# Decay attention and two feed-forward products on one core: order of scalings, weight loads, reads of h, and who stores

## The chip, the core and the metric

The kernel runs on one core of a Trainium2 chip. The core has a matrix engine (TensorE; PE in the profile, PEld for its weight loads), three engines for elementwise work (VectorE, DVE; ScalarE, ACT; GpSimd, POOL) and SyncE (SP), which here only issues DMAs. Each engine works through its own instructions in order and waits at semaphores for the others; DMAs run beside them. The metric is the time of one execution on the device in microseconds, given as the median of several runs.

## The reference

Inputs are float64 arrays in memory for the weights that are unpacked below; the result is float32.

```python
scores = q @ k.T / sqrt(64)                      # 4 x 8 heads, 576 positions, 64 wide
cum    = cumsum(log(clip(f, 1e-4, 1)))
scores = where(causal, -1e9, scores + cum[:, None] - cum[None, :])
attn   = softmax(scores)                         # + 1e-9 under the division
x      = (attn @ v), heads side by side          # 2304 tokens x 512
h      = x @ w_in                                # 512 -> 2048
g      = h * tanh(softplus(h))                   # Mish
y      = g @ w_out                               # 2048 -> 512
out    = max(y @ w1, y @ w2, y @ w3) @ w_out2    # 512 -> 768 -> 512
```

## The kernel before, in words

Products are made in three matmuls of rounded halves (`mm3`: high x high, high x low, low x high), so each operand is first split into a high half (a rounding copy) and a low half (a subtraction), by `split`. Weights lie in memory as 64-bit numbers; `load_f32` brings both 32-bit words of each and puts a float32 together with four DVE steps (lines 156, 159, 162, 166; for w_in a fifth step, line 153, runs on ACT). The raw words have two buffers (`wr`).

Attention goes through 16 pairs of heads (4 batches x 4 pairs), each in two units (`g` 0: the first 256 query rows, `g` 1: the other 320). `load` issues the DMAs of one pair: q, k, v and the cumulated decay, which is spread over the partitions (`cb`), and masks copies of it with three selects on POOL. `prep` splits and transposes q and k. `scores` makes the scores of a unit's tiles (4, or 5 with the last 64 rows of both heads as one tile `P_None`), subtracts decay and finds the minimum on DVE, takes exponentials and sums on ACT; when all tiles are done, two small DVE steps make the reciprocals of the sums and POOL scales the tiles. `av`, one unit later, transposes P (`pp`), splits it (`TA`, `TB`), multiplies by v and stores the result to `x_d` in blocks of 256 tokens.

The first product, `h_steps`, is woven into it: as soon as a block of x is complete, `load_x` reads and splits it, and for each of 8 slices of w_in (`fp`) 24 matmuls make a tile of h, which ACT or DVE in turn copies (`he`, three buffers) and SP stores to `h_d`. Slices of w_in come from `load_w_in`, two groups a slice. When attention is over, 24 of the 72 tiles of h are still to be made, and `load_w_out` unpacks w_out beside them.

The second product goes over 5 blocks of h (four of 512 tokens, one of 256) and, in each, over 16 parts of 128 rows: `load_g` reads a part, applies Mish on ACT, copies the high half on ACT and subtracts on DVE; four buffers each for `g`, `gh`, `gl`. After the last part ACT and DVE copy the four tiles of y (`ze`) and SP stores them to `z_d`. The weights of the third stage (`load_w2`) are unpacked beside it. The third stage then takes the rest of the time.

Order: the program is laid out once, when it is built. A planner goes through the traced instructions by priority (the place in which they were traced; `tc.high_priority(n)` puts them n places forward) and by its own estimate of when inputs and buffers are there, and so fixes the order of each engine and of each DMA queue. Attention is traced with 3000 places (`AHEAD`) of priority. On the chip an instruction whose input is late holds up whatever stands behind it on its engine.

Of the kernel before, what the change touches and what calls it, by code (L numbers as in the profile page):

```python
# [9 lines left out]
F32 = mybir.dt.float32  # L10
# [57 lines left out]
def tile_decay_attention__mish_ff__max3_ff(  # L68
# [74 lines left out]

    def load_f32(pool, srcs, bufs=None, abs_eng="dve", raw="wr"):
# [4 lines left out]
        for i, src in enumerate(srcs):  # L149
            nc.sync.dma_start(r[:, i].rearrange("p n w -> p (n w)"), src.bitcast(I32))  # L150
# [118 lines left out]
    def load(b, hp):  # L269
# [14 lines left out]
        for n, src, dst in ((2, 0, 5), (1, 3, 2), (1, 4, 4)):  # L284
            nc.gpsimd.affine_select(
                out=c2[:, :, dst:dst + n, :], in_=c2[:, :, src:src + n, :], pattern=[[0, 2], [0, n], [-1, 128]],
                compare_op=ALU.is_ge, fill=-1e30, base=0, channel_multiplier=1,
            )
# [4 lines left out]
        nc.gpsimd.tensor_tensor(out=c4[:, 512:S], in0=c4[:, 512:S], in1=mask4, op=ALU.add)  # L293
# [16 lines left out]
    def prep(J):  # L310
# [35 lines left out]
        split_raw(J["vs"], raw[2], "act")  # L346
        J.update(q=(qh, ql), q4=last, k=kk)
# [13 lines left out]
    def scores(J, g):  # L361
# [11 lines left out]
        made = []  # L373
        for ci, (h, qt) in enumerate(tiles):
# [12 lines left out]
            for pi, (c0, w) in enumerate([(0, wd)] if qt < 4 else [(0, 288), (288, 288)]):  # L387
# [6 lines left out]
                    scale=-scale, scalar=(3e38 if pi == 0 else mn[:, ci:ci + 1]),  # L394
                    op0=ALU.add, op1=ALU.min, accum_out=mn[:, ci + pi:ci + pi + 1],
                )
            cl = ci + (qt == 4)
            nc.scalar.activation(  # L398
                Pt, Pt, AF.Exp, scale=-1.0, bias=mn[:, cl:cl + 1], accum_out=sm[:, ci:ci + 1],
            )  # L400
        nt = len(tiles)
        nc.vector.tensor_scalar(rr[:, :nt], sm[:, :nt], 1e-9, None, op0=ALU.add)
        nc.vector.reciprocal(rr[:, :nt], rr[:, :nt])  # L403
        for ci, Pt in enumerate(made):
            nc.gpsimd.tensor_scalar(Pt, Pt, rr[:, ci:ci + 1], 1.0, op0=ALU.mult, op1=ALU.mult)  # L405
        return P

    def av(J, g, P):
# [86 lines left out]
    def h_steps():  # L495
# [9 lines left out]
        for n, (i, fp) in enumerate(order):  # L505
# [48 lines left out]
    at.close()  # L554

# [51 lines left out]
    def load_g(ib, fp, a):  # L607
        n = blocks1[ib][1]
        g = gp_.tile([128, n], F32, name="g", tag="g")
        nc.sync.dma_start(g, h_d[ib][fp][:, a, :])  # L610
        nc.scalar.activation(g, g, AF.Mish)  # L611
        gh = gp_.tile([128, n], F32R, name="gh", tag="gh")
        gl = gp_.tile([128, n], F32R, name="gl", tag="gl")
        split(gh, gl, g, "act", "dve")
        return gh, gl

    wgen3 = load_w2()
    todo = [(ib, fp, a) for ib in range(len(blocks1)) for fp in range(NFP) for a in range(2)]
    ahead = [load_g(*todo[0]), load_g(*todo[1])]
    for step, (ib, fp, a) in enumerate(todo):  # L620
# [3 lines left out]
        g = ahead.pop(0)  # L624
        if step + 2 < len(todo):
            ahead.append(load_g(*todo[step + 2]))
        final = fp == NFP - 1 and a == 1
# [97 lines left out]
```

## Time and profile before

| | us |
|---|---|
| median of 3 runs | 1039.22 (1038.8 to 1040.48) |
| the profiled execution | 1036.78 |
| its span, first to last instruction | 1034.9 |
| TensorE busy / weight loads | 957.5 / 844.8 |
| VectorE busy | 509.5 |
| ScalarE busy | 425.6 |
| GpSimd busy | 379.9 |

The profile gives for each engine when it was busy and, for idle time before an instruction, what ended it (the releaser). Matmuls overlap, so a busy TensorE is not one at its peak. The granted clock of TensorE is a share of 2.4 GHz; it has two levels, 1.0 and 0.5. The rows below are from this execution; L123 is a line of the kernel.

### The profile page before, as it was taken

The numbers are of one execution on the slowest core, as the hardware profiler recorded it, in microseconds if no ns is written. First come the engines' busy times: TensorE is split into PE (matmuls) and PEld (weight loads), VectorE is DVE, ScalarE is ACT, GpSimd is POOL, SyncE is SP. The second block draws the span as 40 slices with busy tenths as digits, with TensorE's granted clock in tenths as the row PEclk, the third lists the DMA queues.
The fourth block names the chain that finished last, engine by engine and source line by source line (L and its number), as shares of the span: only waits on it lengthen the run. The fifth ranks groups of instructions, "written<-read, shape, count | busy, mean of one in ns | idle before, by whom it ended". The sixth has DMA issues, their size and how long they took to land.

```text
span 1034.9 us, 15873 instructions
## 1 busy us (share of the span) xinstructions
PE 957.5 (93%) x5756; PEld 844.8 (82%) x5756; DVE 509.5 (49%) x1103; ACT 425.6 (41%) x936; POOL 379.9 (37%) x437
## 2 busy tenths in 40 slices
PE   4777789989998999899699989998999999999998
PEld 4655679989997999799688768778988888888886
DVE  4798885554555555599855776652211111111110
ACT  5777666565656566441133444434211211211111
POOL 6676784445445542365432423320111001011010
PEclk8888889999998999999899999998999999999999
DMA  6644544345344431485545555643300100200101
GB/s 158 175 145 143 174 155 129 120 131 150 119 129 120 139 107 63 146 285 168 175 141 195 180 185 163 203 134 102 103 21 1 61 21 1 82 1 1 41 0 41
DMA packets 106445, 119.15 MB, mean 115 GB/s; under 512 B 33984, under 2 KB 79552, under 8 KB 106368
## 3 DMA queue, kind: packets, MB, share of 16 engines
q1 hardware_dynamic: 106368, 118.15, 37.0%
q8 instruction: 45, 0.74, 0.3%
q14 instruction: 32, 0.26, 0.1%
HBM read 85.01 MB, written 33.10 MB: 114 GB/s over the span
## 4 chain that ended last, share of the span: by engine, by line
PE 54%; DMA 18%; DVE 17%; issue 4%; ACT 3%; POOL 3%; SPq 2%; DVEq 0%; POOLq 0%; ACTq 0%
PE g L179 7%; PE g L178 7%; PE g L177 7%; DMA wr<-in_moe_w_dram 5%; PE h L177 4%; PE h L178 4%; PE h L179 4%; DMA wr<-in_moe_w_out_dram 4%; DVE wt L162 3%; PE av L437 3%; PE pp L424 3%; PE sc L357 3%; DMA cb<-cum_d 3%; PE o L177 2%; PE o L179 2%
## 5 line engine op out<-in xcount | busy, mean ns | idle before, releaser
L177 PE MATMUL h<-xh,wi 128*128 128x256 f32 x576 | 168.5, 294 | 13.0 <-ACT he L527 7.9
L178 PE MATMUL h<-xl,wi 128*128 128x256 f32 x576 | 167.4, 291 | 1.9 <-POOL xl L142 1.9
L179 PE MATMUL h<-xh,wi 128*128 128x256 f32 x576 | 166.9, 290 | 0.0
L142 POOL TENSOR_TENSOR hl<-mx,hh 128x512 fp32r<-128x512 f32 x27 | 36.5, 1352 | 279.1 <-ACT hh L136 279.1
L177 PE MATMUL g<-yh,wm 128*128 128x512 f32 (+1 forms) x360 | 134.3, 373 | 0.0
L179 PE MATMUL g<-yh,wm 128*128 128x512 f32 (+1 forms) x360 | 134.3, 373 | 0.0
L178 PE MATMUL g<-yl,wm 128*128 128x512 f32 (+1 forms) x360 | 134.3, 373 | 0.0
L177 PE MATMUL y<-gh,wo 128*128 128x512 f32 (+1 forms) x320 | 118.6, 375 | 6.9 <-ACT gh L136 5.0
L177 PEld LDWEIGHTS h<-xh,wi 128*128 128x128 f32 x576 | 112.1, 195 | 15.2 <-ACT he L527 8.8
L178 PE MATMUL y<-gl,wo 128*128 128x512 f32 (+1 forms) x320 | 119.0, 373 | 2.9 <-DVE gl L142 2.8
L179 PE MATMUL y<-gh,wo 128*128 128x512 f32 (+1 forms) x320 | 118.2, 371 | 0.0
L178 PEld LDWEIGHTS h<-xl,wi 128*128 128x128 f32 x576 | 112.5, 195 | 3.2 <-POOL xl L142 2.1
L179 PEld LDWEIGHTS h<-xh,wi 128*128 128x128 f32 x576 | 112.2, 195 | 0.4
L611 ACT ACTIVATE g<-g 128x512 f32<-128x512 f32 (+1 forms) x80 | 46.8, 588 | 123.9 <-DMA g<-h_d 117.4
L681 DVE TENSOR_TENSOR mx<-g,mx 128x512 f32<-128x512 f32 x27 | 18.7, 692 | 156.3 <-PE g L179 156.3
L424 PE MATMUL pp<-ident,P 128*128 128x128 f32 x320 | 69.9, 314 | 21.9 <-POOL P L405 19.8
L398 ACT ACTIVATE P<-P,mn 128x128 f32<-128x128 f32 (+3 forms) x128 | 71.2, 557 | 39.2 <-DVE mn L392 38.5
L178 PEld LDWEIGHTS g<-yl,wm 128*128 128x128 f32 x360 | 67.9, 189 | 13.3
L179 PEld LDWEIGHTS g<-yh,wm 128*128 128x128 f32 x360 | 67.9, 189 | 13.2
L177 PEld LDWEIGHTS g<-yh,wm 128*128 128x128 f32 x360 | 67.9, 189 | 13.1
L405 POOL TENSOR_SCALAR P<-P,rr 128x128 f32<-128x128 f32 (+3 forms) x128 | 68.0, 550 | 25.7 <-DVE rr L403 12.5
L177 PEld LDWEIGHTS y<-gh,wo 128*128 128x128 f32 x320 | 61.3, 192 | 18.4 <-ACT gh L136 6.4
(101 smaller groups left out, 1982.9 us busy)
## 6 DMA issues: line engine op xcount, KB each, us to landing
h_d<-he SPq DMA_DIRECT2D x72, 256.0 KB, 3.5
g<-h_d SPq DMA_DIRECT2D x64, 256.0 KB, 3.2
wr<-in_moe_w_out_dram SPq DMA_DIRECT2D x22, 512.0 KB, 4.0
wr<-in_moe_w_dram SPq DMA_DIRECT2D x24, 384.0 KB, 3.2
cb<-cum_d SPq DMA_DIRECT2D x64, 128.0 KB, 3.2
wr<-in_moe_w_in_dram SPq DMA_DIRECT2D x32, 256.0 KB, 3.5
cb<-cum_d SPq DMA_DIRECT2D x32, 144.0 KB, 3.6
xr<-x_d SPq DMA_DIRECT2D x9, 512.0 KB, 4.0
```

What stands on the lines that cost most here:

```text
L142: eng.tensor_tensor(out=dst_lo, in0=src, in1=dst_hi, op=ALU.subtract)
L162: nc.vector.scalar_tensor_tensor(out=ti, in0=hi, scalar=-0x40000000, in1=ti, op0=ALU.bitwise_and, op1=ALU.bitwise_or,)
L177: nc.tensor.matmul(ps, wh, xh, start=start, stop=False, skip_group_check=True)
L178: nc.tensor.matmul(ps, wh, xl, start=False, stop=False, skip_group_check=True)
L179: nc.tensor.matmul(ps, wl, xh, start=False, stop=stop, skip_group_check=True)
L357: nc.tensor.matmul(o, lhs, rhs, start=n == 0, stop=n == len(mms) - 1, skip_group_check=True)
L398: nc.scalar.activation(Pt, Pt, AF.Exp, scale=-1.0, bias=mn[:, cl:cl + 1], accum_out=sm[:, ci:ci + 1],)
L405: nc.gpsimd.tensor_scalar(Pt, Pt, rr[:, ci:ci + 1], 1.0, op0=ALU.mult, op1=ALU.mult)
L424: nc.tensor.transpose(pp[:, n * 128:n * 128 + 128], Pt[:, k0:k0 + 128], ident)
L437: nc.tensor.matmul(avp[h][:, off:off + w], vl, T[:, i, c:c + w], start=kt == 0 and i == 0 and not (g == 0 and h == 1), stop=last and i == ...
L611: nc.scalar.activation(g, g, AF.Mish)
L681: nc.vector.tensor_tensor(out=mx, in0=g[1], in1=mx, op=ALU.max)
```

## The change

- The identity matrix and its rounded copy are traced with 9000 places of priority.
- `load_f32`: while attention runs, the DMAs of a weight group are ordered, on SP's queue, behind the last store of `av` that was traced before them (`pace`, `tc.issue_after`). This concerns w_in alone; the list is emptied when attention is over. By the driving loop the groups are traced two at a time from the 7th to the 14th step, that is, behind the stores of units 5 to 12.
- The selects and the masked addition on `cb` move from the end of `load` to the end of the same pair's `prep`, half a pair later.
- `scores`: the tile `P_None` comes first in its unit; reciprocals and scalings come in two parts, with 400 places of priority. Columns of the minima are counted through.
- `he` and `ze`: what ACT copies, ACT's own queue stores; what DVE copies, SP stores, as before.
- `load_g`: traced with 3000 places of priority and three parts ahead in place of two; tiles always 512 wide. In the block of 256 tokens one load brings two parts.

```diff
     ident = const.tile([128, 128], F32, name="ident")
-    make_identity(nc, ident)
-    identr = const.tile([128, 128], F32R, name="identr")
-    nc.vector.tensor_copy(identr, ident)
+    with tc.high_priority(3 * AHEAD):
+        make_identity(nc, ident)
+        identr = const.tile([128, 128], F32R, name="identr")
+        nc.vector.tensor_copy(identr, ident)
...
+        with tc.issue_after(pace[-1].ins) if pace else ExitStack():
+            for i, src in enumerate(srcs):
+                nc.sync.dma_start(r[:, i].rearrange("p n w -> p (n w)"), src.bitcast(I32))
...
         split_raw(J["vs"], raw[2], "act")
+        c2, c4 = J["cb"]
+        for n, src, dst in ((2, 0, 5), (1, 3, 2), (1, 4, 4)):
+            nc.gpsimd.affine_select(
+                out=c2[:, :, dst:dst + n, :], in_=c2[:, :, src:src + n, :], pattern=[[0, 2], [0, n], [-1, 128]],
+                compare_op=ALU.is_ge, fill=-1e30, base=0, channel_multiplier=1,
+            )
+        nc.gpsimd.tensor_tensor(out=c4[:, 512:S], in0=c4[:, 512:S], in1=mask4, op=ALU.add)
...
-        tiles = [(h, qt) for h in range(2) for qt in ((0, 1) if g == 0 else (2, 3))]
-        if g == 1:
-            tiles.append((None, 4))
+        tiles = [(None, 4)] if g == 1 else []
+        tiles += [(h, qt) for h in range(2) for qt in ((0, 1) if g == 0 else (2, 3))]
+        def scale_rows(part):
+            cs = slice(part[0], part[-1] + 1)
+            with tc.high_priority(400):
+                nc.vector.tensor_scalar(rr[:, cs], sm[:, cs], 1e-9, None, op0=ALU.add)
+                nc.vector.reciprocal(rr[:, cs], rr[:, cs])
+                for ci in part:
+                    nc.gpsimd.tensor_scalar(made[ci], made[ci], rr[:, ci:ci + 1], 1.0, op0=ALU.mult, op1=ALU.mult)
...
+            if ci == 2 - (g == 0):
+                scale_rows(list(range(ci + 1)))
+        scale_rows(list(range(3 - (g == 0), len(tiles))))
...
-            nc.sync.dma_start(x_d[blk][:, J["hp"], off:off + n], xt[:, done:done + n])
+            pace[:] = [nc.sync.dma_start(x_d[blk][:, J["hp"], off:off + n], xt[:, done:done + n])]
...
                 nc.vector.tensor_copy(he, h)
+                queue = nc.sync
             else:
                 nc.scalar.activation(he, h, AF.Copy)
+                queue = nc.scalar
-            nc.sync.dma_start(h_d[ib][fp][:, :, off:off + BLK], he)
+            queue.dma_start(h_d[ib][fp][:, :, off:off + BLK], he)
...
+        if n == BLK2:
+            nc.sync.dma_start(g, h_d[ib][fp][:, a, :])
+        else:
+            nc.sync.dma_start(g.rearrange("p (a n) -> p a n", a=2), h_d[ib][fp][:])
...
-    ahead = [load_g(*todo[0]), load_g(*todo[1])]
+    with tc.high_priority(AHEAD):
+        ahead = [load_g(*t) for t in todo[:3]]
...
-        if step + 2 < len(todo):
-            ahead.append(load_g(*todo[step + 2]))
+        if step + 3 < len(todo):
+            with tc.high_priority(AHEAD):
+                ahead.append(load_g(*todo[step + 3]))
...
                     nc.vector.tensor_copy(ze, y[j])
+                    nc.sync.dma_start(z_d[ib][:, j, :], ze)
                 else:
                     nc.scalar.activation(ze, y[j], AF.Copy)
-                nc.sync.dma_start(z_d[ib][:, j, :], ze)
+                    nc.scalar.dma_start(z_d[ib][:, j, :], ze)
```

## Rows read from the trace of the kernel before

**Rows 1.** Busy us by stretch: length, PE, PEld, DVE, ACT, POOL, clock, DMA.
```profile
35.00:150.00 115.00, 88.14 (x528) 74.63 (x529) 97.34 (x223) 81.83 (x198) 83.56 (x94) 0.84 0.51 154
150.00:220.00 70.00, 68.78 (x571) 67.73 (x571) 41.43 (x122) 42.23 (x107) 34.53 (x49) 1.00 0.47 141
...
523.00:730.00 207.00, 197.23 (x946) 165.05 (x946) 118.48 (x224) 82.13 (x155) 59.30 (x57) 0.98 0.50 160
```
**Rows 2.** The same for tile wt (unpacking) alone: length, DVE, ACT, POOL, clock, DMA.
```profile
35.00:81.00 46.00, 17.76 (x24) 7.86 (x12) 8.29 (x6) 0.85 0.55 160
...
81.00:194.00 113.00, 35.02 (x40) 12.85 (x20) 14.37 (x10) 0.89 0.50 151
```
**Rows 3.** Tile x_d, 30 to 81.5 us: issues, ns min/median/max, first to last start.
```profile
L462 SPq DMA_DIRECT2D x_d<-xt x7: 335/376/584, 33.0 to 80.9; - x7
```
**Rows 4.** Chain of waits, 35 to 81 us: shares by engine and line.
```profile
by line: DMA wr<-in_moe_w_in_dram 16.6%; issue 8.9%; PE sc L357 8.5%; DVE P L392 7.9%; DVE wt L162 7.6%; DVE wt L166 7.5%; DVE TB L432 5.1%; DMA cb<-cum_d 4.6%; SPq L150 4.4%; PE pp L424 3.9%; DVE P_None L392 2.7%; DVE wt L159 2.5%; DVE xt 
```
**Rows 5.** Busy us by stretch, columns as in rows 1.
```profile
81.00:194.00 113.00, 96.68 (x687) 88.70 (x688) 85.49 (x204) 73.54 (x179) 74.86 (x89) 0.89 0.50 151
```
**Rows 6.** Tile wt, 35 to 150 us: ns min/median/max, first to last start.
```profile
L156 DVE TENSOR_SCALAR wt<-wt x15: 412/427/1592, 40.0 to 144.4; 128x512 f32<-128x512 f32 x15
...
L162 DVE SCALAR_TENSOR_TENSOR wt<-wr,wt x15: 676/714/1948, 40.9 to 148.1; 128x512 int32<-128x512 int32 x15
```
**Rows 7.** Tile rr, whole span, columns as in rows 6.
```profile
L402 DVE TENSOR_SCALAR rr<-sums x32: 156/172/602, 17.9 to 419.7; 128x4 f32<-128x4 f32 x16, 128x5 f32<-128x5 f32 x16
```
**Rows 8.** Busy us by stretch, columns as in rows 1.
```profile
235.00:430.00 195.00, 187.96 (x1522) 183.02 (x1520) 106.44 (x309) 116.36 (x290) 85.42 (x121) 0.98 0.38 115
```
**Rows 9.** Waits of PE, 35 to 150 us: us in total, times, longest.
```profile
PE pp L424 <- POOL P L405: 13.1, 11, 3.4
```
**Rows 10.** Waits, whole span, columns as in rows 9.
```profile
POOL cb L285 <- DMA cb<-cum_d: 34.6, 8, 8.5
```
**Rows 11.** Order of time: start, us, engine, line, what [idle before <- releaser].
```profile
327.25 0.47 PE L424 MATMUL pp<-ident,P 128*128 128x128 f32 x1 [3.64 <-POOL P L405]
```
**Rows 12.** Busy us by stretch, columns as in rows 1.
```profile
502.00:516.00 14.00, 6.34 (x29) 6.00 (x28) 11.72 (x17) 2.17 (x4) 6.42 (x7) 0.63 0.43 129
...
324.70:331.50 6.80, 3.97 (x16) 2.92 (x16) 1.36 (x3) 1.20 (x3) 6.33 (x13) 0.50 0.55 182
703.50:710.30 6.80, 5.02 (x23) 5.02 (x24) 0.94 (x3) 2.75 (x8) 0.00 (x0) 0.50 0.64 219
```
**Rows 13.** Order of time at the change of stage, columns as in rows 11.
```profile
495.17 0.62 ACT L136 ACTIVATE gh<-g 128x512 fp32r<-128x512 f32 x1
...
504.90 0.68 DVE L142 TENSOR_TENSOR gl<-g,gh 128x512 fp32r<-128x512 f32 x1
...
508.70 0.63 ACT L611 ACTIVATE g<-g 128x512 f32<-128x512 f32 x1 [9.69 <-DMA g<-h_d]
...
509.86 0.58 PE L177 MATMUL h<-xh,wi 128*128 128x256 f32 x1 [7.66 <-ACT he L527]
```
**Rows 14.** Waits, 430 to 523 us, columns as in rows 9.
```profile
ACT he L527 <- DMA h_d<-he: 15.1, 5, 3.7
```
**Rows 15.** Waits of PE, 523 to 730 us, columns as in rows 9.
```profile
PE y L177 <- ACT gh L136: 5.0, 3, 2.0
PE y L178 <- DVE gl L142: 2.8, 4, 1.2
PE y L177 <- ACT ze L639: 1.8, 1, 1.8
```
**Rows 16.** Tile he, up to 430 us, columns as in rows 6.
```profile
L529 SPq DMA_DIRECT2D h_d<-he x48: 513/552/1423, 132.4 to 422.9; - x48
```
**Rows 17.** Order of time at the start, columns as in rows 11.
```profile
5.87 1.54 POOL L142 TENSOR_TENSOR qk<-rawk,qk 128x576 fp32r<-128x576 f32 x1 [3.56 <-DVE qk L140]
...
7.63 0.60 PE L319 MATMUL tr<-identr,qk 128*128 128x128 f32 x3 [7.63 <-DVE identr L109]
```
**Rows 18.** Waits of SP's queue, 523 to 730 us, columns as in rows 9.
```profile
SPq L610 <- DVE gl L142: 48.9, 49, 4.7
```

More of the change, by code (lines that the diff above doesn't have):

```diff
@@ L142, in split @@
         eng.tensor_tensor(out=dst_lo, in0=src, in1=dst_hi, op=ALU.subtract)
+    pace = []
     def load_f32(pool, srcs, bufs=None, abs_eng="dve", raw="wr"):
@@ L148, in load_f32 @@
         r = pool.tile([128, m, n, 2], I32, name=raw, tag=raw, bufs=bufs if raw == "wr" else 1)
-        for i, src in enumerate(srcs):
-            nc.sync.dma_start(r[:, i].rearrange("p n w -> p (n w)"), src.bitcast(I32))
+        with tc.issue_after(pace[-1].ins) if pace else ExitStack():
+            for i, src in enumerate(srcs):
+                nc.sync.dma_start(r[:, i].rearrange("p n w -> p (n w)"), src.bitcast(I32))
         lo, hi, ti = r[:, :, :, 0], r[:, :, :, 1], t.bitcast(I32)
@@ L283, in load @@
             nc.sync.dma_start(c2[:, h, 3:5, :], src[:, 2:4])
[L284 to L288, printed above, removed]
         ld(rv, v, b, hp, False)
@@ L292, in load @@
             nc.sync.dma_start(c4[rows], cum_d[r + h:r + h + 1, :].to_broadcast([64, S]))
-        nc.gpsimd.tensor_tensor(out=c4[:, 512:S], in0=c4[:, 512:S], in1=mask4, op=ALU.add)
         return dict(b=b, hp=hp, cb=(c2, c4), vs=vs[i % 2])
@@ L393, in scores @@
                     out=like(Pt[:, c0:c0 + w]), in0=like(sc[:, :w]), in1=cb[pi],
-                    scale=-scale, scalar=(3e38 if pi == 0 else mn[:, ci:ci + 1]),
-                    op0=ALU.add, op1=ALU.min, accum_out=mn[:, ci + pi:ci + pi + 1],
+                    scale=-scale, scalar=(3e38 if pi == 0 else mn[:, col - 1:col]),
+                    op0=ALU.add, op1=ALU.min, accum_out=mn[:, col:col + 1],
                 )
-            cl = ci + (qt == 4)
+                col += 1
             nc.scalar.activation(
-                Pt, Pt, AF.Exp, scale=-1.0, bias=mn[:, cl:cl + 1], accum_out=sm[:, ci:ci + 1],
+                Pt, Pt, AF.Exp, scale=-1.0, bias=mn[:, col - 1:col], accum_out=sm[:, ci:ci + 1],
             )
[L401 to L405, printed above, removed]
+            if ci == 2 - (g == 0):
+                scale_rows(list(range(ci + 1)))
+        scale_rows(list(range(3 - (g == 0), len(tiles))))
         return P
@@ L554, in tile_decay_attention__mish_ff__max3_ff @@
     at.close()
+    pace.clear()
     sb = ExitStack()
@@ L607, in load_g @@
     def load_g(ib, fp, a):
+        g = gp_.tile([128, BLK2], F32, name="g")
+        gh = gp_.tile([128, BLK2], F32R, name="gh")
+        gl = gp_.tile([128, BLK2], F32R, name="gl")
         n = blocks1[ib][1]
-        g = gp_.tile([128, n], F32, name="g", tag="g")
-        nc.sync.dma_start(g, h_d[ib][fp][:, a, :])
+        if n == BLK2:
+            nc.sync.dma_start(g, h_d[ib][fp][:, a, :])
+        else:
+            nc.sync.dma_start(g.rearrange("p (a n) -> p a n", a=2), h_d[ib][fp][:])
         nc.scalar.activation(g, g, AF.Mish)
-        gh = gp_.tile([128, n], F32R, name="gh", tag="gh")
-        gl = gp_.tile([128, n], F32R, name="gl", tag="gl")
         split(gh, gl, g, "act", "dve")
-        return gh, gl
+        return [(t, (gh[:, i * n:(i + 1) * n], gl[:, i * n:(i + 1) * n])) for i, t in enumerate([a] if n == BLK2 else [0, 1])]
     wgen3 = load_w2()
-    todo = [(ib, fp, a) for ib in range(len(blocks1)) for fp in range(NFP) for a in range(2)]
-    ahead = [load_g(*todo[0]), load_g(*todo[1])]
+    todo = [(ib, fp, a) for ib, (_, n) in enumerate(blocks1) for fp in range(NFP) for a in range(n // BLK)]
+    with tc.high_priority(AHEAD):
+        ahead = [load_g(*t) for t in todo[:3]]
     for step, (ib, fp, a) in enumerate(todo):
@@ L623, in tile_decay_attention__mish_ff__max3_ff @@
             y = [yps.tile([128, n], F32, name=f"y{j}", tag="y") for j in range(KD)]
-        g = ahead.pop(0)
-        if step + 2 < len(todo):
-            ahead.append(load_g(*todo[step + 2]))
-        final = fp == NFP - 1 and a == 1
-        for j in range(KD):
-            js = slice(j * 128, (j + 1) * 128)
-            mm3(y[j], (wo[fp][:, 0, a, js], wo[fp][:, 1, a, js]), g, fp == 0 and a == 0, final)
+        parts = ahead.pop(0)
+        if step + 3 < len(todo):
+            with tc.high_priority(AHEAD):
+                ahead.append(load_g(*todo[step + 3]))
+        for t, g in parts:
+            final = fp == NFP - 1 and t == 1
+            for j in range(KD):
+                js = slice(j * 128, (j + 1) * 128)
+                mm3(y[j], (wo[fp][:, 0, t, js], wo[fp][:, 1, t, js]), g, fp == 0 and t == 0, final)
         if step % 2:
```

1 line of the change is left out of this document (added).

## The prediction

> **What bounds the kernel now.** I read the busy time by stage first [rows 1]. The reader is to see three things. From 35 to 150 us TensorE (PE) is busy 88 of 115 us at a mean granted clock of 0.84, while VectorE (DVE) is busy 97 of 115: attention runs there beside the unpacking of w_in, and DVE is the bound. From 150 us to attention's end PE is nearly full (68.8 of 70 us). In 523 to 730 us, the second product, it is busy 197 of 207. Between the last two it multiplies the last blocks of h while DVE unpacks w_out, and stands still once. So time can be won only where PE idles or runs at the lower of its two clocks: the early part, single stalls, the change of stage, the second product. The third stage, from 730 us on, no edit touches.
>
> Next I read who waited for whom in each stage, and then the chain of waits and the order of time at each stall. The profiled execution took 1036.8 us, span 1034.9; the median of the runs is 2.4 us above it, so I sum against 1036.8 and add 2.4.
>
> **1. w_in's loads behind attention's stores.** There are 16 groups of two loads. Each is unpacked by four DVE steps, (17.76 + 35.02) / 16 = 3.3 us a group [rows 2]. Now they start right behind the first unit of attention; afterwards two groups stand behind each of the stores of units 5 to 12. Units 2 to 5, whose stores lie behind the one at 33 us and up to 81 us [rows 3], lose this work: 17.8 us of DVE. The chain of waits of that stretch gives the same bound: 16.6 + 7.6 + 7.5 + 4.4 + 2.5 = 38.6% of 46 us is w_in's [rows 4]. I take 12 of the 17.8, since attention's own latencies then come forward. The work does not vanish. It goes to units 6 to 13 (81 to 194 us), where DVE is busy 85.5 of 113 us [rows 5]; that becomes 85.5 + 17.8 + 2.8 (see 2) = 106. At the share that DVE reaches from 35 to 150 us, 97.3 / 115 = 0.846, 106 us want 125, 12 more; at 106 / 113 = 0.94 none. I take 8, nearer the measured share. Net -4, from -18 (nothing given back) to +4 (8 won, 12 given back). Behind each paced load on SyncE's queue (SP) stand attention's next loads and stores; they wait when a load waits for its buffer, as they do now.
>
> How long the steps take depends on what runs beside them: the same step takes 412 to 1592 ns, another 676 to 1948 [rows 6]. The Trainium skill (SBUF — State Buffer, Who interferes with whom) says that VectorE in its two-port mode and GpSimd take one port pair in turn, and the second waits out the whole instruction. The spread in the trace fits that; the rule speaks against this edit, since the steps move into units in which GpSimd (POOL) scales and splits as much as before.
>
> **2. Scalings put forward.** A unit's scaling now waits for all its tiles; afterwards it comes in two parts, with priority, and the widest tile is made first. That adds an addition and a reciprocal on DVE a unit, two small steps of 172 ns [rows 7]: 0.34 us, 11 in 32 units, 2.8 in units 6 to 13 (counted above). Later DVE is half idle (106 of 195 us [rows 8]), which hides the rest; without that cover it costs 8 us. What can be won is PE's waits for P: 13.1 us in 35 to 150 us [rows 9], where DVE and not PE is the bound. I take -2, from -6 to +3.
>
> **3. Selects moved from the load to the end of the preparation.** POOL waited 34.6 us in 8 places for cb's DMA with the select at its head [rows 10], and P's scalings are queued behind it. Mostly PE had other work. Once, at 323.6 us, it had none: 3.64 us [rows 11], and the clock then stood at 1.2 GHz (0.50) for 6.8 us, as it did at 703.5 us [rows 12], in which PE loses at most half, 3.4. Moved half a pair later, the select finds its data landed. Late next is the softmax itself, so I take -5, from -7 to 0.
>
> **4. The change of stage at 502 us.** PE waits 7.66 us for a copy of h by ScalarE (ACT), which stands 9.69 us on a Mish whose load of g is late. That load waited for a buffer, freed by a subtraction that came at 504.90 on DVE, behind w_out's steps, though its input was made at 495.17 [rows 13]. The clock in 502 to 516 us is 0.63 [rows 12], (1 - 0.63) x 14 = 5.2 us lost. Together 12.9 us. The change gives the reads of h and all that hangs on them, subtraction included, 3000 places of priority, ahead of w_out's steps on DVE and of ACT's copies of h; and the stores of those copies leave SP, where they stood behind loads that wait for DVE (ACT waited 15.1 us in 5 places for such stores to free a buffer [rows 14]). So this stall should go. Late next is w_out itself: DVE still has to unpack its 16 groups before the second product can run. I take -10, from -13 to +3.
>
> **5. The second product.** In 523 to 730 us PE waits 5.0 us for gh, 2.8 for gl, 1.8 for a copy of y [rows 15], and 6.8 us run at the lower clock from 703.5 [rows 12], worth 3.4: 13.0 us. That last fall lies in the final block, 256 columns wide, where each load serves half as many columns. Afterwards one load brings two of its halves: 16 loads, Mish, copies and subtractions become 8 wide ones. The depth of reading is three in place of two, but with the same four buffers. Copies of y now stand behind Mish of higher priority on ACT. I take -7, from -13 to +4.
>
> **6. ACT stores its own copies.** The 46 stores of ACT's copies of h and 10 of y leave SP. One issue took 552 ns there beside attention [rows 16]; no row shows one on ACT, so I take SP's. Half of the 48 up to 430 us are ACT's: 24 x 0.55 = 13 us of ACT, which is busy 116 of 195 us there [rows 8]; behind each stand exponentials and copies. Hidden but for about 1 us; bounds 0 and +13. What it may bring is counted in 4.
>
> The Trainium skill (DMA: Bandwidth & Descriptors, Issuing engines are not separate DMA queues) says that issuing from several engines saves only the sequencer's time of issue. By that alone edit 6 would bring nothing; the trace shows a second thing, the 15.1 us in which ACT waited for its own stores. The sum is the same by either.
>
> **7. Identity put forward.** PE's first transposes start at 7.63 us, released by the identity; but the halves of k, which they need as well, end at 7.41 [rows 17]. 0, at most -0.2.
>
> **The sum.** -4 - 2 - 5 - 10 - 7 + 1 = -27; 1036.8 - 27 = 1009.8, and with 2.4 about 1012.
>
> **The rivals.** *Slower: h waits for w_in.* Each engine's order is fixed when the program is built, by estimated durations. If w_in comes later than the plan holds, matmuls of h stand in front of attention's on PE and everything stops; until now w_in was in before most of h began. A group's 3.3 us against the sum of the shortest (412 and 676 ns [rows 6], and two more like them), 2.2, is 1.1 us late; two groups a slice of w_in and 8 slices make 18 us; four stalls, each with 3.4 us lost to the clock as in part 3, add 14. That is +32 in place of -4: 1036.8 + 32 - 23 = 1046, with 2.4 about 1048. It decides once PE loses over 23 us there. For it: the spread of rows 6. Against it: six groups, three slices, stand before unit 8's store, and only then are two blocks of x complete.
>
> *The reads do not come forward.* SP waited 48.9 us in 49 places for the subtraction that frees a buffer of g [rows 18]. If the four buffers and not the order are the limit, 4 and 5 bring nothing: -10 in all, 1029. Against it: at the change of stage the subtraction could have run 9 us earlier and stood in DVE's order.
>
> *More is won.* With 4 and 5 at their ends (-26), 1 to 3 at two thirds of theirs (-21) and 6 at +1: -46, near 993.
>
> **How the numbers follow.** Forecast, 1002 to 1022: 0.50. Reads not forward, or other gains partly given back, 1022 to 1037: 0.20. Gains and costs cancel, within 0.2% (about what a measurement of this kernel can tell from no change, 1037.1 to 1041.3): 0.05. Slower: 0.12. More, below 1002: 0.13. Faster is 0.50 + 0.20 + 0.13 = 0.83. The range from 994 to 1040 leaves out the slower rival and about half of the case of more, 0.18. The likeliest's own range is 1002 to 1022.
>
> **What would show it.** Right: no w_in load before unit 5's store; units 2 to 5 at 9 us each in place of 12; DVE at 0.85 or more from there to 190 us; no wait of POOL's selects for cb; no PE gap over 3 us between 430 and 530; the last block without a fall of the clock. Wrong: PE idle before matmuls of h with w_in's subtraction or copy as releaser; ACT still waiting on g's loads with copies of h behind; longer gaps at the copies of y.

## The result, and the profile after

The changed kernel takes 1026.06 us (median of 4 runs, 1021.8 to 1027.96) against 1039.01 for the kernel before beside it: a ratio of 0.9871 [0.9839, 0.9903], 13 us faster. The profiled execution took 1024.48 us, span 1022.5. The sign was right, and the time lies in the stated range (994 to 1040 us), but outside the likeliest one (1002 to 1022): 27 us were forecast, and about half of that came.

The ends of the stages, read from the last TensorE (PE) instruction of each in the two traces (us; the first two rows are starts of stores, the last ends with ScalarE's last copy of the output), show where the time went:

| | before | after | difference | forecast |
|---|---|---|---|---|
| store of unit 5 | 80.9 | 68.2 | -12.7 | -12 |
| store of unit 13 | 192.3 | 192.3 | 0.0 | |
| attention's last product | 428.9 | 410.9 | -18.0 | parts 1, 2, 3, 6: -10 |
| from there to h's last product | 92.9 | 86.4 | -6.5 | part 4: -10 |
| from there to y's last product (second product) | 208.0 | 219.4 | **+11.4** | part 5: -7 |
| from there to the last copy of the output | 302.0 | 302.6 | +0.6 | 0 |

Up to h's last product 24.5 us are won, more than the 20 forecast. Then nearly half of it is lost in the second product. Busy time by stretch, after (length, PE, PEld, DVE, ACT, POOL, clock, DMA), against [rows 1, 5, 8, 12]:

```profile
35.00:150.00 115.00, 93.17 (x576) 80.19 (x576) 95.90 (x237) 79.94 (x196) 79.91 (x94) 0.82 0.51 148
35.00:81.00 46.00, 39.66 (x271) 34.44 (x271) 34.43 (x97) 36.65 (x94) 30.02 (x45) 0.93 0.46 129
81.00:194.00 113.00, 97.50 (x675) 89.24 (x674) 98.25 (x238) 75.10 (x178) 77.00 (x85) 0.85 0.56 169
235.00:411.00 176.00, 172.89 (x1426) 170.27 (x1424) 104.44 (x309) 108.24 (x272) 82.91 (x115) 0.99 0.38 115
487.00:501.00 14.00, 12.54 (x68) 11.78 (x69) 12.57 (x18) 3.55 (x6) 6.16 (x7) 0.76 0.42 142
497.00:717.00 220.00, 204.83 (x951) 166.78 (x950) 119.07 (x227) 80.02 (x140) 64.19 (x63) 0.97 0.47 153
```

The pacing did what it says. The unpacking (tile wt; length, DVE, ACT, POOL) has left the early stretch and stands in the next, against [rows 2]; VectorE (DVE) is busy 98.25 of 113 us there, 0.87:

```profile
35.00:81.00 46.00, 3.57 (x3) 1.31 (x2) 0.00 (x0) 0.93 0.46 129
81.00:194.00 113.00, 46.73 (x62) 19.52 (x30) 21.85 (x16) 0.85 0.56 169
```

The stall at the change of stage stayed. Order of time after, against [rows 13]:

```profile
472.71 0.62 ACT L137 ACTIVATE gh<-g 128x512 fp32r<-128x512 f32 x1
...
483.79 0.68 DVE L143 TENSOR_TENSOR gl<-g,gh 128x512 fp32r<-128x512 f32 x1
484.50 0.33 SPq L631 DMA_DIRECT2D g<-h_d  x1
...
487.29 0.63 ACT L634 ACTIVATE g<-g 128x512 f32<-128x512 f32 x1 [11.14 <-DMA g<-h_d]
487.82 0.58 ACT L542 ACTIVATE he<-h 128x512 f32<-128x512 f32 x1
488.45 0.58 PE L182 MATMUL h<-xh,wi 128*128 128x256 f32 x1 [6.75 <-ACT he L542]
```

The chain is the old one: the subtraction's input was made by 473.3, it runs at 483.79 among w_out's steps, only then does its buffer come free for the read at 484.50, and Mish, with h's copy behind it on ScalarE (ACT), waits 11.14 us. PE waits 6.75 us where it waited 7.66. The Trainium skill (PSUM — Partial Sum Buffer, Engine vs sequencer instructions) calls VectorE's queue a strict FIFO; the trace agrees, the subtraction standing there 10.5 us with its input ready.

PE's waits in the second product (us in total, times, longest), against [rows 15], are of another kind than before: the subtractions lead.

```profile
PE y L183 <- DVE gl L143: 10.5, 12, 2.2
PE y L182 <- ACT gh L137: 3.4, 4, 1.5
PE y L182 <- ACT ze L664: 0.7, 1, 0.7
PE y L182 <- DVE ze L661: 0.5, 1, 0.5
```

What makes the subtractions late is seen in one turn of VectorE and SyncE's queue (SP) there:

```profile
506.84 0.33 SPq L155 DMA_DIRECT2D wr<-in_moe_w_dram  x1
...
510.51 0.36 DVE L160 TENSOR_SCALAR wt<-wr 128x384 int32<-128x384 int32 x1 [3.10 <-DMA wr<-in_moe_w_dram]
510.90 0.36 DVE L161 TENSOR_SCALAR wt<-wt 128x384 f32<-128x384 f32 x1
511.30 0.36 DVE L164 TENSOR_SCALAR wt<-wt 128x384 int32<-128x384 int32 x1
511.57 0.69 DVE L143 TENSOR_TENSOR gl<-g,gh 128x512 fp32r<-128x512 f32 x1
512.18 0.55 DVE L167 SCALAR_TENSOR_TENSOR wt<-wr,wt 128x384 int32<-128x384 int32 x1
512.76 0.56 DVE L171 SCALAR_TENSOR_TENSOR wt<-wr,wt 128x384 int32<-128x384 int32 x1
513.24 0.68 DVE L143 TENSOR_TENSOR gl<-g,gh 128x512 fp32r<-128x512 f32 x1
513.35 0.33 SPq L155 DMA_DIRECT2D wr<-in_moe_w_dram  x1
```

The third stage's weights have one buffer for their raw words (tile `wr1` in the kernel; the profile leaves the number out), where the other weights have two, and all five unpacking steps of a group run on VectorE. So a load is issued at 506.84, VectorE's first step finds it at 510.51 (3.67 us), the five steps with a subtraction among them end at 513.32 (2.81 us), and only then is the next load issued, at 513.35: 6.51 us a turn. Two subtractions stand in a turn, so PE gets operands for two steps of the loop in 6.51 us. It uses them up in 5.44 (2.72 us a step where nothing waits). VectorE is half idle, and yet it looks like the pace. The waits for loads on VectorE are there in both kernels, first the kernel before from 523 to 730 us, then the changed one from 497 to 717:

```profile
DVE wt L155 <- DMA wr<-in_moe_w_dram: 35.5, 19, 3.3
DVE wt L155 <- DMA wr<-in_moe_w_out_dram: 12.0, 5, 4.0
```

```profile
DVE wt L160 <- DMA wr<-in_moe_w_dram: 57.0, 22, 4.1
DVE wt L160 <- DMA wr<-in_moe_w_out_dram: 15.7, 6, 4.5
```

From the starts of the first steps behind h's end a turn takes 6.33 us in the mean before (27 turns) and 6.67 after (28). Not every turn has two subtractions: after, 23 have two, four have three and one has one. So far this is a reading; it became theory 5 below.

### The profile page after: what moved, and what is told of

The parts are those of the page before. It is cut to its first block, busy times and chain, and to the rows that moved or that the text cites. A ratio compares the mean times of both kernels' runs of the same rounds, so it can differ in the third digit from the quotient of the medians.

```text
span 1022.5 us, 15879 instructions
## 1 busy us (share of the span) xinstructions
PE 955.2 (93%) x5756; PEld 840.6 (82%) x5756; DVE 511.9 (50%) x1159; ACT 422.0 (41%) x920; POOL 378.3 (37%) x437
## 4 chain that ended last, share of the span: by engine, by line
PE 57%; DMA 18%; DVE 17%; issue 2%; ACT 2%; SPq 2%; POOL 1%; DVEq 0%; ACTq 0%; POOLq 0%
PE g L183 7%; PE g L184 7%; PE g L182 7%; DMA wr<-in_moe_w_dram 7%; DMA wr<-in_moe_w_out_dram 5%; PE h L183 4%; PE h L184 4%; PE h L182 4%; PE av L451 4%; PE sc L363 4%; DVE wt L171 3%; PE pp L438 3%; DVE wt L167 3%; PE o L182 2%; PE o L184 2%; PE o L183 2%
## 5 line engine op out<-in xcount | busy, mean ns | idle before, releaser
L183 PE MATMUL y<-gl,wo 128*128 128x512 f32 (+1 forms) x320 | 121.6, 380 | 10.5 <-DVE gl L143 10.5
L182 PE MATMUL y<-gh,wo 128*128 128x512 f32 (+1 forms) x320 | 120.5, 378 | 4.6 <-ACT gh L137 3.4
L184 PE MATMUL y<-gh,wo 128*128 128x512 f32 (+1 forms) x320 | 119.5, 375 | 0.0
L634 ACT ACTIVATE g<-g 128x512 f32<-128x512 f32 x72 | 45.5, 632 | 138.5 <-DMA g<-h_d 128.3
L183 PEld LDWEIGHTS y<-gl,wo 128*128 128x128 f32 x320 | 61.8, 193 | 26.5 <-DVE gl L143 17.0
L183 PEld LDWEIGHTS g<-yl,wm 128*128 128x128 f32 x360 | 68.2, 189 | 13.4
L184 PEld LDWEIGHTS g<-yh,wm 128*128 128x128 f32 x360 | 68.2, 189 | 13.2
L438 PE MATMUL pp<-ident,P 128*128 128x128 f32 x320 | 64.4, 303 | 11.9 <-POOL P L388 11.7
```

The costliest lines, as they stand in the source:

```text
L182: nc.tensor.matmul(ps, wh, xh, start=start, stop=False, skip_group_check=True)
L183: nc.tensor.matmul(ps, wh, xl, start=False, stop=False, skip_group_check=True)
L184: nc.tensor.matmul(ps, wl, xh, start=False, stop=stop, skip_group_check=True)
L438: nc.tensor.transpose(pp[:, n * 128:n * 128 + 128], Pt[:, k0:k0 + 128], ident)
```

## The experiments

"Second product" is the time from h's last product to y's last; "late half" the time from attention's last product to y's last (before 300.9, after 305.8), which doesn't depend on whether a stall falls before or behind h's end. Both are from the profiled execution of each run.

**Parts alone.** Four kernels, each the kernel before with one part of the change. Reads put forward and joined (and nothing else):

> The kernel before with part 4/5 alone: reads of h with priority, three ahead, and the joined reads of the last block. Theory 1 (these reads lengthen the second product, because their subtraction now stands inside the unpacking of the third stage's weights on VectorE): attention ends within 2 us of 431 as before, the second product takes 215 to 221 us in place of 208, time 1043 to 1050. Theory 2 (the reads gain what was forecast or nothing, the loss comes from another part): second product 200 to 209 us, time 1022 to 1039.

ScalarE's own stores (the same for the copies of y):

```diff
+                queue = nc.sync
...
+                queue = nc.scalar
...
-            nc.sync.dma_start(h_d[ib][fp][:, :, off:off + BLK], he)
+            queue.dma_start(h_d[ib][fp][:, :, off:off + BLK], he)
```

> The kernel before with part 6 alone: ScalarE stores its own copies of h and y. Theory 1: worth little either way, 1035 to 1040; the stall of 7 us at the change of stage stays. Theory 2 (the stores on ScalarE's queue delay Mish and so the second product): second product 213 us or more, time 1043 or more.

The pacing of w_in's loads (the lines with `pace` of the diff):

> The kernel before with part 1 alone: w_in's loads behind attention's stores. Theory 1 (the work moves to units in which VectorE has no room, so most of the early gain is given back, as forecast): unit 5 stored 10 to 13 us sooner, attention ends 2 to 6 us sooner, time 1033 to 1037. Theory 2 (the early gain is kept): attention ends 9 to 14 us sooner, time 1025 to 1030.

Scalings and selects, with the identity put forward:

> The kernel before with parts 2, 3 and 7: scalings and identity put forward, selects moved into the preparation. Theory 1 (forecast 7 us, and TensorE's wait at 324 us goes): attention ends 5 to 9 us sooner, time 1030 to 1034. Theory 2 (the gain of attention in the changed kernel is the pacing's alone): attention ends within 2 us of 431, time 1037 to 1041.

| part alone | ratio | attention ends | second product | late half |
|---|---|---|---|---|
| reads | 1.0028 [1.0008, 1.0049] | -3.0 | 215.2 | 303.5 |
| stores | 1.0124 [1.0083, 1.0166] | -3.3 | 218.0 | 312.1 |
| pacing | 0.9996 [0.9975, 1.0017] | -6.7 | 221.3 | 307.8 |
| scalings, selects | 0.9976 [0.9959, 0.9993] | -7.1 | 211.3 | 303.7 |

Up to attention's end the parts nearly add up: -3.0 - 3.3 - 6.7 - 7.1 = -20.1, against -18.0 together. Behind it each loses, 2.6 to 11.2 us of late half, and in whole times the parts don't add up: by their ratios they cost some 13 us in all, where the whole change wins 13. The second product is longer in all four, by 3 to 13 us, also with the pacing and with the scalings and selects, which don't touch its code. So it needn't be the joined reads that lengthen it.

Against what was expected: with the reads the second product fits theory 1 and the time theory 2. The stores fit theory 2 in both numbers, but its reason, a late Mish, isn't seen: VectorE waits 31.3 us for high halves there, 35.9 in the kernel before, and 72.1 us for loads, 47.5 in the kernel before. The pacing alone stored unit 5 only 7.1 us sooner, where 10 to 13 was expected, and attention ended between the two theories' ranges. Scalings and selects came out as theory 1 had them.

**The reads, the buffer, the order on PE.** Theory 1 is still that the reads' priority makes the second product long. Theory 3 is that the single buffer sets the pace. Of the stall at the change of stage, theory A holds that it is a loss by itself, theory B that w_out's unpacking covers it. Three kernels from the changed one: without the reads put forward and joined; with two buffers for the raw words (`raw="wr1"` becomes `raw="wr"` in load_w2); with all products of y behind h's last:

```diff
-                    mm3(
+                    last_h[:] = mm3(
...
-                mm3(y[j], (wo[fp][:, 0, t, js], wo[fp][:, 1, t, js]), g, fp == 0 and t == 0, final)
+                with tc.issue_after(last_h[-1].ins):
+                    mm3(y[j], (wo[fp][:, 0, t, js], wo[fp][:, 1, t, js]), g, fp == 0 and t == 0, final)
```

and a fourth with the last two together.

> The changed kernel with load_g and its calls as they were (no priority, two ahead, no joined reads). Theory 1 (the forward reads lengthen the second product): second product back at 206 to 210 us, time 1010 to 1016. Theory 3 (the second product goes at the pace at which the third stage's weights come through their single raw buffer, one group for two parts of h; the pace depends on how each plan lays the subtractions between the unpacking steps, not on the reads' priority): pace of weight groups still 6.2 us or more, second product 214 us or more, time 1023 to 1031.

> The changed kernel with the raw words of the third stage's weights in the two buffers that w_out's had, in place of one of their own. Theory 3: a load no longer waits for the unpacking of the one before it, the second product follows TensorE, 198 to 206 us in place of 219, time 1006 to 1014. Theory 1 (priority of reads and the order on VectorE are the cause): second product stays at 214 us or more, time 1021 to 1028.

> The changed kernel with the matmuls of the second product ordered behind the last matmul of h on TensorE, so that no buffer of g comes free before h is done and no Mish beyond the fourth stands between ScalarE's copies of h. Theory A (such a Mish, waiting for its read, causes the stall of 6.75 us at the change of stage): no gap over 2 us between 430 us and h's end, h ends 8 to 10 us sooner on TensorE's own work less 29 matmuls moved behind it (7 us), time 1016 to 1024. Theory B (the chain of weight unpacking from attention's end sets the end of the second product, and TensorE's stall there is covered by it): the gap goes, h ends sooner, and the second product ends where it did, time 1023 to 1030.

> The edits of b2 and b3 together. Theory A with theory 3: 996 to 1006. Theory B with theory 3: as b2, 1006 to 1014. Theory 1: 1015 or more.

| changed kernel and | ratio | median us | second product | late half |
|---|---|---|---|---|
| no reads forward | 0.9794 [0.9766, 0.9821] | 1014.58 | 219.6 | 300.2 |
| two buffers | 0.9847 [0.9819, 0.9876] | 1020.11 | 216.9 | 300.7 |
| y behind h | 0.9846 [0.9815, 0.9876] | 1020.25 | 231.5 | 302.2 |
| both | 0.9885 [0.9854, 0.9915] | 1023.11 | 234.4 | 305.1 |

Without the reads the kernel is faster, and yet its second product is as long as with them: theory 1 falls. Attention ends 4.0 us sooner in it, and h's end follows in 80.6 us in place of 86.4. With y behind h the stall goes (PE's waits between attention's and h's end fall from 7.9 to 0.8 us, h ends at 477.2, 20.1 us earlier), and the second product takes 12.1 of these back; the late half is 3.6 shorter and the time in theory A's range, so A and B stay undecided. With two buffers VectorE's waits for loads all but vanish (72.8 to 5.0 us), a turn takes 4.17 us, and still the second product takes 216.9, where 198 to 206 was expected: theory 3 falls as it stood. The order in that trace says why:

```profile
532.45 0.35 DVE L160 TENSOR_SCALAR wt<-wr 128x384 int32<-128x384 int32 x1
532.72 0.99 DVE L143 TENSOR_TENSOR gl<-g,gh 128x512 fp32r<-128x512 f32 x1
533.64 1.17 DVE L161 TENSOR_SCALAR wt<-wt 128x384 f32<-128x384 f32 x1
...
536.31 0.35 DVE L160 TENSOR_SCALAR wt<-wr 128x384 int32<-128x384 int32 x1
536.58 0.99 DVE L143 TENSOR_TENSOR gl<-g,gh 128x512 fp32r<-128x512 f32 x1
```

Here the planned order has mostly one subtraction in a turn (in 18 of 28). This turn takes 3.86 us (532.45 to 536.31), and PE needs a subtraction every 2.72. Both edits together took 1023.11 us, no better than either alone.

**Order by hand, first try; the same program again; the unpacking taken away.** Theory 4: the order of subtractions and steps on VectorE decides. The first edit orders a group's first step behind the subtraction made last before it:

```diff
-            nc.vector.tensor_scalar(ti, hi, 0x7FFFFFFF, None, op0=ALU.bitwise_and)
+            with tc.issue_after(subs[-1].ins) if subs else ExitStack():
+                nc.vector.tensor_scalar(ti, hi, 0x7FFFFFFF, None, op0=ALU.bitwise_and)
...
-        split(gh, gl, g, "act", "dve")
+        subs[:] = [split(gh, gl, g, "act", "dve")]
```

> The changed kernel, in which VectorE starts to unpack each of the third stage's groups of weights only behind the subtraction of g that was made last before it in the program; nothing is left out. Theory 4 (the order on VectorE decides: in the changed kernel subtractions of the first blocks stand between the unpacking steps of one group, behind a step that waits for a weight load, and a group of two steps then takes 6.4 to 6.9 us in place of 5.4): no subtraction stands inside a group any more, the second product from the last product of h to the last product of y takes 198 to 208 us in place of 219, and the time is 1005 to 1014 us. Rival (the order only goes along with the length; TensorE's own sequence or the edges of the blocks decide): 214 us or more, time 1021 to 1028.

> The changed kernel without the forward and joined reads of h (the run of 1014.6 us), with the same order for the unpacking of the third stage's weights. Theory 4: second product 200 to 208 us in place of 219.6, time 996 to 1005. Rival: 216 us or more, time 1012 to 1017.

> The changed kernel once more, nothing edited. If the plan decides how long the second product takes: 219 us within 1 us, time 1022 to 1028. If chance in the timing on the chip decides it: a length anywhere from 208 to 221, and a time that differs by 5 us or more.

> The changed kernel, in which the weights of the third stage are loaded and unpacked only behind the last store of y, so that the second product runs without that work beside it; nothing is left out, and the third stage starts that much later (the whole time some 80 to 120 us longer, which is not the question). Theory 4, and any theory by which the unpacking beside the second product lengthens it: second product 195 to 203 us, without waits for gl beyond 2 us in all. Rival (the reads of h or the edges of the blocks lengthen it): 214 us or more, with the waits at the edges as before.

The first try gave 0.9876 [0.9828, 0.9924] with the reads (second product 222.4) and 0.9822 [0.9774, 0.9869] without (220.8). It decided nothing about theory 4: it kept a subtraction from falling behind the steps, but not the next one from coming in among them, and the traces still show one there in 23 of 30 and 21 of 29 groups.

The changed kernel once more took 1027.58 us, 0.9904 [0.9872, 0.9936], with the same order on every engine and a second product of 225.7 in place of 219.4, outside both expected ranges. The two executions that were profiled took 1029.77 and 1024.48 us. So the same plan varies by 6 us in this stage; differences of that size between single traces carry no cause.

With the third stage's weights loaded only behind y, PE had no wait over 0.15 us in the whole second product, and it took 193.1 us:

```profile
491.00:684.00 193.00, 192.89 (x942) 163.48 (x940) 53.76 (x77) 86.10 (x142) 3.68 (x2) 1.00 0.35 112
```

(The rest of that kernel is longer, as intended: 1111.92 us in its one run.) What the second product of the changed kernel takes beyond some 193 us, 26 us, comes with the loading and unpacking beside it. Reads, edges of blocks and copies of y cost nothing when it is gone.

**Order and buffers.** Theory 5: the pace is a turn of VectorE, its wait for the load included, over the subtractions that the plan put into it. The second edit fixes the turn: two subtractions, then the five steps, by ordering the subtractions behind a group's last step (`lasts`) as well, beside the first edit's order; with two buffers in three of the kernels.

```diff
-                        "pool", "pool", raw="wr1",
+                        "pool", "pool", raw="wr",
...
-        split(gh, gl, g, "act", "dve")
+        with tc.issue_after(lasts[-1].ins) if subs else ExitStack():
+            last = split(gh, gl, g, "act", "dve")
+        pend[:] = [last]
...
+            subs[:] = pend
             next(wgen3, None)
```

> The changed kernel with two buffers for the raw words of the third stage's weights, and VectorE's order in the second product written by hand: two subtractions of g, then the five steps of one group, in turn; nothing is left out. Theory 5 (a turn of VectorE, one group with its wait for the load and the subtractions planned into it, brings TensorE's operands slower than the 5.44 us in which it uses up two of them: 6.1 to 6.5 us for two with one buffer, 3.9 us for one with two buffers in the planned order): with no wait for the load and two subtractions to a turn it takes some 4 to 5 us, the waits for gl fall to 4 us or less, the second product takes 196 to 206 us in place of 219, and the time is 1002 to 1012 us. Rival (the edges of the blocks, the joined reads or what is left over from the stage before make its length): 213 us or more, time 1016 to 1028.

> The same two edits, buffers and order, in the changed kernel without the forward and joined reads of h. Theory 5: second product 196 to 206 us in place of 219.6, time 992 to 1002. Rival: 213 us or more, time 1009 to 1018.

> The changed kernel with the same order by hand, but one buffer for the raw words, as it has. By theory 5 a turn is what the trace of the changed kernel shows where it already has this order, 5.9 us (from 583.38 to 589.32 us) against TensorE's 5.44, 0.5 us lost a turn, less what the stock of buffers takes: second product 205 to 213 us, time 1012 to 1021. If the wait for the load, and not the order, sets the length: 217 us or more, time 1022 to 1028. If the order alone does: 196 to 204 us, time 1000 to 1010.

> The kernel before with the same two edits, buffers and order, and nothing of the change. By theory 5 its second product too runs at VectorE's pace: 196 to 204 us in place of 208, time 1025 to 1034. Rival (the second product is long only in the changed kernel, by something that came with the change): 206 to 210 us, time 1037 to 1042.

| kernel and edits | ratio | median us | second product | late half |
|---|---|---|---|---|
| changed, buffers, order | **0.9649** [0.9610, 0.9689] | 998.03 | 194.9 | 278.3 |
| changed without reads, buffers, order | 0.9680 [0.9640, 0.9721] | 1001.95 | 208.4 | 283.9 |
| changed, order, one buffer | 0.9812 [0.9765, 0.9859] | 1015.10 | 220.6 | 297.8 |
| before, buffers, order | 0.9927 [0.9896, 0.9958] | 1027.98 | 195.1 | 290.4 |

These runs bear out theory 5; the first and the fourth kernel's second products are even below what it expected. The second kernel's, 208.4, is above its 196 to 206, though the time lies in its range: h ends 8.5 us sooner there than in the first, and PE waits 8.3 us behind it. A turn in the first of these kernels, and its second product (length, PE, PEld, DVE, ACT, POOL, clock):

```profile
510.00 0.69 DVE L143 TENSOR_TENSOR gl<-g,gh 128x512 fp32r<-128x512 f32 x1 [1.29 <-ACT gh L137]
510.61 0.35 DVE L162 TENSOR_SCALAR wt<-wr 128x384 int32<-128x384 int32 x1
510.99 0.36 DVE L163 TENSOR_SCALAR wt<-wt 128x384 f32<-128x384 f32 x1
511.39 0.36 DVE L166 TENSOR_SCALAR wt<-wt 128x384 int32<-128x384 int32 x1
511.78 0.56 DVE L169 SCALAR_TENSOR_TENSOR wt<-wr,wt 128x384 int32<-128x384 int32 x1
512.37 0.56 DVE L173 SCALAR_TENSOR_TENSOR wt<-wr,wt 128x384 int32<-128x384 int32 x1
513.22 0.85 DVE L143 TENSOR_TENSOR gl<-g,gh 128x512 fp32r<-128x512 f32 x1 [0.29 <-ACT gh L137]
515.44 0.69 DVE L143 TENSOR_TENSOR gl<-g,gh 128x512 fp32r<-128x512 f32 x1 [1.37 <-ACT gh L137]
```

```profile
494.00:689.00 195.00, 194.99 (x957) 165.29 (x956) 132.07 (x226) 81.72 (x141) 60.19 (x63) 1.00 0.56 174
```

The turn from 510.00 to 515.44 is 5.44 us: now VectorE waits for ScalarE's copies, and these for PE's consumption, so PE sets the pace. It is busy 194.99 of 195.00 us at the full clock. VectorE's wait for loads has gone from 72.8 us to

```profile
DVE wt L162 <- DMA wr<-in_moe_w_dram: 0.5, 1, 0.5
```

GpSimd's splits (60.19 us busy, 64.19 in the changed kernel) and the DMA traffic (174 GB/s, 153 in the changed kernel) run beside it as before, so neither of these alone sets the length. In the kernel before the same edits bring the second product from 208.0 to 195.1, so it was already paced by VectorE there:

```profile
523.00:718.00 195.00, 194.34 (x956) 164.68 (x955) 123.61 (x224) 83.01 (x156) 55.19 (x58) 1.00 0.52 168
```

Neither edit does it alone: two buffers left 216.9, and the order with one buffer 220.6, where 205 to 213 was expected; VectorE still waits 44.2 us for loads there. (In that last kernel h ended 9 us earlier and 5.7 us of the wait moved behind it; the late half fell by 8.0, and the time lay where it was expected.) The Trainium skill (Trainium Kernel Development and Optimization, Best Practices) advises two buffers, so that transfers lie beside work; here the second buffer alone brought 2.5 us of the second product, less than one program varies by, and 24.5 together with the order.

**What the reads and the stall are worth then.** Two more: the kernel before with buffers, order and the reads alone; and the run of 998.03 us with y behind h.

> The kernel before with two buffers, the order by hand, and of the change only the reads of h (put forward, joined in the last block). In it the second product no longer runs at VectorE's pace, so that what the reads bring by themselves is seen, against the kernel before with buffers and order alone (1028.0 us, 290.4 us from attention's end to the last product of y). If parts 4 and 5 of the prediction were right about what the reads bring and only the pace hid it: 10 to 17 us less, 273 to 280 us, time 1011 to 1018. If the reads bring a few us at the edges and the stall at the change of stage stays, as it did in the changed kernel: 3 to 8 us less, time 1020 to 1025. If they bring nothing: within 2 us of it.

> The run of 998.0 us (changed kernel, two buffers, order by hand) with all products of y behind the last product of h on TensorE. If the stall at the change of stage (7.6 us of waits there, 3.4 us lost to the clock) is a loss by itself: 278 us from attention's end to the last product of y become 266 to 272, time 987 to 993. If the unpacking of w_out stands behind it anyway: 275 to 281, time 995 to 1001.

The reads give 0.9850 [0.9806, 0.9894], 1021.57 us, late half 284.4: 6.0 us less than buffers and order alone, as the middle case had it. All of it lies ahead of h's end (95.3 to 89.5 us from attention's end); the second product takes 195.1 without the reads and 194.9 with them. In the pair without them and with them on the changed kernel it is 5.6 (283.9 to 278.3); by the whole times the two pairs give 6.4 and 3.9 us. Their worth is some 4 to 6 us, not 17, and with the pace unmended it isn't to be seen: there the reads cost 0.3% alone, and the changed kernel is 0.8% faster without them (0.9794 against 0.9871). With y behind h the kernel takes 997.77 us, 0.9617 [0.9575, 0.9658], the same as without that edit, and the late half is 282.5, a little longer than thought; PE's waits ahead of h's end go from 7.6 to 1.2 us, those in the second product from none to 9.5. So the stall at the change of stage is no loss by itself, as theory B had it: VectorE ends w_out's unpacking at 496.6 us, 493.8 without that edit, and PE, done with h at 482.5, stands 3.6 us for a subtraction until 497.2.

## Why the prediction was right or wrong

**The step that failed is part 5.** It read PE's waits for gh, gl and the copies of y [rows 15] and the last fall of the clock [rows 12] as delays of reading, 13.0 us, that deeper, earlier and joined reads would cut by 7, or at worst lengthen by 4. The sum of the excess was right: 208.0 - 195.1 = 12.9 us with buffers and order mended. Its cause was wrong. Nothing asked why the subtraction was late: VectorE, busy 118 of 207 us [rows 1], has no place in that part, though it stood 47.5 us (35.5 + 12.0) on loads of weights with subtractions queued behind. With that mended the kernel before has its single, narrow reads in the last block as ever, and yet PE waits 0.6 us and the clock doesn't fall (1.00): neither waits nor fall came from the reads, and they bring the second product nothing (195.1 to 194.9). The rows [rows 18] showed SP waiting 48.9 us for subtractions, and the prediction took that for a matter of four buffers. The second product became 11.4 us longer: the waits for gl rose from 2.8 to 10.5 us, all of PE's waits there from 9.7 to 15.2, and the clock was low twice as long, 6.8 us lost in place of 3.4. The last block was to be without a fall of the clock; it had one of 3.4 us at 691.8.

**Why it grew.** A turn went from 6.33 to 6.67 us, the way from a load's issue to the first step from 3.55 to 3.75 in the mean, and 23 of 29 groups have a subtraction among their steps in place of 15 of 28. That this pace binds is shown by the runs with buffers and order; that it lengthened just so much by this change isn't. Without the reads the changed kernel has 15 of 29 such groups and the same 219.6, so that count alone doesn't decide. All kernels with one buffer and a planned order have a late half of 300 to 312 us, and one program twice gave 305.8 and 312.2. Which part of the change moved the order, and how much of the 11.4 us is chance, stays open.

**Part 4** had its cause right and its remedy wrong. It said that the stall comes from a subtraction standing in w_out's steps, and that 3000 places of priority would move it. They did not: it ran 10.5 us after its input was ready, where it had been some 9 before. A sign that it had named for being wrong came with it: ScalarE waits on a load of g with copies of h behind. And with the pace mended the stall proved no loss by itself (997.77 us without it, 998.03 with it). 6.5 of the 10 us came nonetheless: from attention's end to h's, PE's waits fell from 11.7 to 7.9 us, the loss to the clock from 6.8 to 3.4. The rival by which the reads do not come forward, at 1029 (the case from 1022 to 1037), was the nearest, but by luck: it kept parts 1 to 3 as they were and had 4 and 5 at nothing, where the trace has -6.5 and +11.4.

**Part 1** was right in its mechanism: unit 5 was 12.7 us early, and the work came back in units 6 to 13. More was given back by unit 13 than thought, all of it and not 8. But then unit 16 was 12.2 us early again; no run shows why. Alone the pacing brought 6.7 us to attention's end, forecast 4. **Parts 2 and 3** were forecast at -7 and brought 7.1 alone. PE's waits for P from 35 to 150 us fell from [rows 9] to 9.0, and the wait of 3.64 us [rows 11] is gone (from 235 us on the longest is 1.8). "No wait of POOL's selects for cb" was wrong, though the selects (L348) wait for its DMA 12.3 us in place of 34.6 [rows 10]. The masked addition (L352), now last in the preparation, waits 19.0 in place of 2.4:

```profile
POOL cb L352 <- DMA cb<-cum_d: 19.0, 9, 6.0
...
POOL cb L348 <- DMA cb<-cum_d: 12.3, 11, 2.9
```

**Part 6** was costed right, 24 issues of 0.52 us on ACT's queue up to attention's end, 12.5 against 13, hidden:

```profile
L545 ACTq DMA_DIRECT2D h_d<-he x24: 520/521/581, 111.5 to 405.7; - x24
```

ACT's waits for its own stores [rows 14] are gone in the changed kernel. Attention even ended 3.3 us earlier with that part alone. That kernel was the slowest of the four by what it lost behind attention's end, 11.2 us. **Part 7** brought nothing, as said: PE's first transposes start at 7.58 us. The slower rival, h waiting for w_in, did not come: PE is busy 172.89 of 176 us from 235 us on.

## What to carry to other kernels

Where an in-order engine is half idle and yet named as the releaser of the bound engine's waits, look at what it waits for itself, and count what it delivers in one turn of its order against what the bound engine uses up in that time. A single load buffer and a planned order that puts a subtraction behind the wait for a load make a hidden pace. Mend both together: alone the buffers and the order took 5.1 and 8.0 us off the late half here, about what one program varies by (6.4), and both 27.5. While such a pace stands, each part of a change can move the stage by as much as the part is worth (the late half went from 300 to 312 us), so test parts once the pace is mended. That a gain made ahead is always given back isn't so: without the reads the changed kernel kept all 22 us of attention's gain.

## What the runs showed that was not expected

One program, run twice, differed by 6.3 us in the length of one stage with one fixed order on every engine (219.4 and 225.7), while the stage behind it took 302.6 both times. One issue of a store on ScalarE's queue took 0.52 us beside attention and 0.33 at the change of stage (488.43 us). And PE's clock, whose falls the prediction priced singly, stayed at its full level for the whole second product once next to no wait was left (1.00 in place of 0.97 and, in the kernel before, 0.98).
